# Prepare and drain steps of the second batch's attention heads, in an attention and mixture-of-experts kernel

## The chip, the core and the metric

The kernel runs on one core of a Trainium2 chip. The time is device microseconds (us) of one execution. Before the change the median of three executions is 731.03 us (730.82 to 731.37). The engines are named as in the profile: PE (matrix multiply) and PEld (its weight loads), DVE (vector), ACT (scalar), POOL (GpSimd), and SP, which issues nearly all transfers from one queue, in program order.

## What is computed

The reference runs two layers one after the other, on 2 batches of 8 heads with 768 positions of 64 columns:

```python
q_bits = (np.einsum('bhsd,dk->bhsk', q, proj) > 0)
k_bits = (np.einsum('bhsd,dk->bhsk', k, proj) > 0)
mask = q_bucket[:, :, :, None] == k_bucket[:, :, None, :]
scores = np.where(mask, scale * np.matmul(q, k.transpose(0, 1, 3, 2)), -1e9)
x = softmax(scores) @ v            # heads side by side: (1536, 512)
for e in range(4):
    out += p[:, e:e + 1] * (np.maximum(x @ w1[e], 0.0) @ w2[e])
```

The bucket of a position is a 6-bit hash of its row (the signs of its products with `proj`).

## The kernel before

**Heads and steps.** The 16 heads, counted 0 to 15 over both batches (8 to 15 are the second batch), are worked through one after the other, each in six steps, one for each 128 query rows. Step i = 6x + t is row block t of head x. Steps 96 to 108 only drain what is left. A generator (`attention`) emits the stages of a step in the order of the letters `TXSUVMEYNRP` and hands control back after each stage that has a charge. Heads 0 to 8 turn their probabilities on PE (stage T). Heads 9 to 15, which I call light, turn them by a detour: stage X (L490) turns 32x32 blocks on DVE and writes three row blocks together to a scratch in DRAM (`scr`, L496), and stage Y (L507) reads them back with four transfers into a tile `pt`. A head has two such groups of three row blocks, g0 and g1.

**The lags.** Y for g0 of head x stands in step 0 of head x+1 and Y for g1 in step 3 of head x+1. Stage V (L525, 24 matmuls) is the product with v; it needs both `pt` tiles of its head. For a light head it stands 8 steps after the head's last row block, that is in step 1 of head x+2. Stage U copies V's PSUM bank out one step later (ACT L554 for one half, DVE L552 for the other). The pool of `pt` tiles has 3 buffers, and the block-turned tile of g1 takes one of them, so Y for g0 of head x+1 needs a buffer that V of head x gives free. V stands one step behind that Y. Tiles are handed out with semaphores, so this Y simply waits on SP until PE has run V.

**Preparing a head.** `prep_head` prepares head x+1 during the first steps of head x, one piece at stage P of each step. For a light head: step 0 makes the rounded copy `ah` (ACT L330) and three copies of it on POOL; step 1 makes the rest `al` (DVE L333), then the hash: four small matmuls into `hps` (PE L346) and two sign evaluations (ACT L356); step 2 makes the bits (POOL). Heads 2 to 8 do these pieces in steps 1, 2 and 3. Block loads of the next q and k (`tqk`, L206, four transfers) are issued at step 1 of each head.

**The experts.** Once the first batch's attention is done (step 53) the first batch's expert layers start, and the second batch's attention runs between their pieces. There are 8 units, u0 to u7. A unit has 8 first-layer blocks, F0 to F7 (12 matmuls of 384 columns each, L791 to L793; ACT L797 makes `hh`, DVE L798 makes `hl`), and 6 second-layer tiles, G0 to G5 (12 matmuls of 512 columns, L731 to L733; DVE L725). Every weight comes as a 512 KB transfer (L681, issued by `load_w`) into one of two buffers `ws`; DVE rounds it (L699), POOL makes the rest (L692). `split_w` advances by one piece after each block or tile: the w2 of a unit is rounded at F0 to F3 of that unit, and its two transfers are issued after G4 and after G5 of the unit before. The w1 of the next unit is rounded at G0 to G3, its transfers are issued at F4 and F6. All of these share four one-bank PSUM buffers (`ps1`): expert blocks, `hps` and the pv bank. DVE works in program order, so what stands behind a rounding waits with it.

**The pace.** Each expert piece has a charge (1960 for F, 2600 for G), and each attention stage has one (1363 for S, 654 for T, 978 when a head is prepared, 2500 for a drain step). Attention pieces are emitted while their sum is below the experts' sum times 112,404 / 250,240 = 0.449:

```python
for c in (moe_fast if b else moe)(b, b * NU):
    dm += c
    while da < dm * ATT_PACE * n_att / n_moe:
        x = next(att, None)
        ...
        da += x
```

`n_att` counts 1632 = 654 + 978 for each prepared head, while a head's generator hands back only 978. `mixed(b, h)` is true for heads 0 to 8 (`LIGHT_FROM` is 9, `H` is 8).

Of the kernel before, what the change touches and what calls it, by code (L numbers as in the profile page):

```python
# [8 lines left out]
F32 = mybir.dt.float32  # L9
F32R = mybir.dt.float32r  # L10
ACTF = mybir.ActivationFunctionType
ALU = mybir.AluOpType
PSUM = bass.MemoryType.PSUM

P = 128
# [3 lines left out]
SGN_SCALE = float(2**20)  # L19
ATT_PACE = 1.0  # L20
LAG_E = 1
SPLIT_AT = (1, 0)
HASH_AT = (3, 1)
LAG_N = 3
LAG_R = ((6, 4), (7, 6))
LAG_T = 3
LAG_X = 2
LAG_Y = 4
LAG_V = ((4, 6), (8,))
LAST_V = (4, 5)  # L30
LAG_U = (3, 1)
LAG_M = (10, 10)
# [19 lines left out]
def tile_lsh_attention__then__domain_moe(  # L52
# [11 lines left out]
    nc = tc.nc  # L64
    B, H, S, D = q.shape
# [12 lines left out]
    NH = S // 2  # L78
# [3 lines left out]
    MKE = MK + 2 * NB  # L82
    scale = 1.0 / float(D) ** 0.5
# [21 lines left out]
    def one(name):  # L105
        return ps1.tile([P, 512], F32, tag="one", name=name)

    ident = const.tile([P, P], F32, name="ident")
    qk_scale = const.tile([P, 1], F32, name="qk_scale")
    sgn_bias = const.tile([P, 1], F32, name="sgn_bias")  # L110
# [4 lines left out]
    pf = const.tile([P, P - D], F32, name="pf")  # L115
# [6 lines left out]
    def two(t):  # L122
        return t.rearrange("p (a n) -> p a n", a=2)
# [103 lines left out]
    def stack_tiles(b, h):  # L227
        heads[b, h] = tuple(stk.tile([P, S], F32R, tag=n, name=n) for n in ("q1", "al", "ah", "k2"))
        return heads[b, h]

    def copy_pool(dst, src):
        nc.gpsimd.tensor_scalar(out=dst, in0=src, scalar1=1.0, scalar2=1.0, op0=ALU.mult, op1=ALU.mult)
# [7 lines left out]
    def split_half(dst_hi, dst_lo, src):  # L240
        nc.scalar.activation(dst_hi, src, ACTF.Copy, scale=qk_scale)
        nc.vector.scalar_tensor_tensor(
            out=dst_lo, in0=src, scalar=qk_scale, in1=dst_hi.bitcast(F32), op0=ALU.mult, op1=ALU.subtract
        )

    halves = [slice(i * NH, (i + 1) * NH) for i in range(2)]
# [54 lines left out]
    def prep_head(b, h):  # L301
        second = (b, h) == (0, 1)
        q1, al, ah, k2 = stack_tiles(b, h)

        def copies():
            for rows in (slice(0, D), slice(D, P)):
                copy_pool(q1[rows], ah[0:D].bitcast(F32))
            copy_pool(k2[0:D], ah[D:P].bitcast(F32))

        if second:  # L310
            for ps, sl in zip(in_psum, halves):
                split_half(ah[:, sl], al[:, sl], ps[:, :NH])
            copies()
            yield 654
            yield 0
            ps = [one("hps1") for _ in range(2)]
            for j, (w, a) in enumerate(((phi, ah), (plo, ah), (phi, al))):
                for i, sl in enumerate(halves):
                    nc.tensor.matmul(ps[i][:MKE, :NH], w, a[:, sl], start=j == 0, stop=j == 2)
            copy_pool(ah[0:D], al[D:P].bitcast(F32))  # L320
            for i, sl in enumerate(halves):
                nc.scalar.activation(
                    k2[D:MKE, sl], ps[i][D:MKE, :NH], ACTF.Sign, bias=sgn_bias[D:MKE], scale=SGN_SCALE
                )
            yield 978
        else:
            xt = xts.pop((b, h))
            for _ in range(SPLIT_AT[not mixed(b, h)]):
                yield 0
            nc.scalar.activation(two(ah), two(xt), ACTF.Copy, scale=qk_scale)  # L330
            copies()
            yield 0
            nc.vector.scalar_tensor_tensor(  # L333
                out=two(al),
                in0=two(xt),
                scalar=qk_scale,
                in1=two(ah).bitcast(F32),
                op0=ALU.mult,
                op1=ALU.subtract,
            )  # L340
            copy_pool(ah[0:D], al[D:P].bitcast(F32))
            for _ in range(HASH_AT[not mixed(b, h)] - SPLIT_AT[not mixed(b, h)] - 1):
                yield 0
            hps = one("hps")
            for i, sl in enumerate(halves):
                nc.tensor.matmul(  # L346
                    hps[i * D : i * D + MKE - D, :NH],
                    pf[:, : MKE - D],
                    xt[:, sl],
                    start=True,  # L350
                    stop=True,
                    tile_position=(0, i * D),
                )
            for i, sl in enumerate(halves):
                rows = slice(i * D, i * D + MKE - D)
                nc.scalar.activation(  # L356
                    k2[D:MKE, sl], hps[rows, :NH], ACTF.Sign, bias=sgn_bias[rows], scale=SGN_SCALE
                )
            if not mixed(b, h):
                yield 978  # L360
        nc.gpsimd.tensor_scalar(
            out=al[D:MKE],
            in0=k2[D:MKE].bitcast(F32),
            scalar1=1.0,
            scalar2=bit_mul[D:MKE],
            op0=ALU.add,
            op1=ALU.mult,
        )
        copy_pool(k2[MQ:MQE], al[MK:MKE].bitcast(F32))
        yield 978 if mixed(b, h) and not second else 0  # L370

    xhi = {}
    xlo = {}
# [17 lines left out]
    def mixed(b, h):  # L391
        return b * H + h < LIGHT_FROM
# [35 lines left out]
    rows = {}  # L428
# [151 lines left out]
    def v_lags(b, h):  # L580
        return LAST_V if (b, h) == (0, H - 1) else LAG_V[not mixed(b, h)]

# [6 lines left out]
    def attention():  # L589
# [3 lines left out]
        def do(op, i):  # L593
# [24 lines left out]
            elif op == "S":  # L618
                if i < n:
                    b, h, t = seq[i]  # L620
                    if t == 0:
                        x = hseq.index((b, h))
                        prep[0] = prep_head(*hseq[x + 1]) if x + 1 < len(hseq) else iter(())
                    stage_s(b, h, t)
                    return 652 + 4270 // NT
# [383 lines left out]
    with tc.manual_schedule():  # L1009
# [6 lines left out]
        i = 0  # L1016
# [57 lines left out]
```

## Time and profile before

| | us |
|---|---|
| median of 3 executions | 731.03 (730.82 to 731.37) |
| the profiled execution, its own time | 729.12 |
| its span, first to last instruction | 727.4 |
| PE busy in that span | 711.5 |
| mean granted clock of PE | 0.997 |

Up to about 130 us the first batch's attention runs, up to about 460 us the first batch's experts with the second batch's attention between them, and then the second batch's experts alone. A row with "[4.67 <-DVE hl L798]" says that the engine stood idle for 4.67 us before this instruction and what released it. "SPq" is SP's queue. [...]

### The profile page before, as it was taken

To read this page: it belongs to the slowest core of one execution; us is meant where nothing else is said; L and a number is where in the kernel's file an instruction comes from. 1 tells how busy PE (TensorE), PEld (TensorE's weight loads), DVE (VectorE), ACT (ScalarE), POOL (GpSimd) and SP (SyncE) were. 2 spreads that over 40 slices of the span, in tenths; PEclk is the share of its full clock that TensorE was granted. 3 is DMA by queue.
4 is the path that set the end of the run, shared out by engine and by line. 5 is a ranking of instruction groups with operands and counts; after the bars stand their busy time and mean duration, and the time that the engine had idled before them with its cause. 6 is when DMAs were issued, how large, how long until landed. Compare 5 with 4: busy or idle time off the path is not lost.

```text
span 727.4 us, 10195 instructions
## 1 busy us (share of the span) xinstructions
PE 711.5 (98%) x3786; PEld 602.5 (83%) x3786; DVE 483.0 (66%) x800; ACT 296.6 (41%) x588; POOL 303.0 (42%) x283
## 2 busy tenths in 40 slices
PE   8999999999999999999979999999999999999998
PEld 6766766887978878798768889898998989899896
DVE  6898898456857566668524333986768576685863
ACT  6888888432433324323111111543425334352440
POOL 6359577413354253424213243933434243342420
PEclk9999999999999999999999999999999999999999
DMA  5323253227858869786466121142113221112202
GB/s 146 66 46 88 58 117 80 39 77 187 232 138 225 234 175 236 212 267 195 134 199 163 37 71 67 59 146 87 59 59 87 58 87 58 59 59 88 87 1 87
DMA packets 88641, 83.05 MB, mean 114 GB/s; under 512 B 53008, under 2 KB 55568, under 8 KB 88592
## 3 DMA queue, kind: packets, MB, share of 16 engines
q1 hardware_dynamic: 87568, 82.08, 41.0%
q8 instruction: 30, 0.49, 0.3%
q10 hardware_dynamic: 1024, 0.33, 0.2%
q14 instruction: 19, 0.16, 0.1%
HBM read 62.68 MB, written 19.71 MB: 113 GB/s over the span
## 4 chain that ended last, share of the span: by engine, by line
PE 88%; DVE 3%; DMA 3%; ACT 2%; POOL 1%; issue 1%; SPq 1%; DVEq 0%; POOLq 0%; ACTq 0%
PE mps L731 12%; PE mps L732 12%; PE mps L733 12%; PE pv L525 8%; PE mps L791 5%; PE mps L792 5%; PE mps L793 5%; PE ptps L470 4%; PE sps L404 4%; PE sps L402 4%; DMA ws<-in_moe_w_dram 3%; PE mps L946 2%; PE mps L942 2%; PE mps L945 2%; PE pd L942 2%; PE pa L946 2%
## 5 line engine op out<-in xcount | busy, mean ns | idle before, releaser
L731 PE MATMUL mps<-w2hi,hh 128*128 128x512 f32 (+1 forms) x388 | 151.0, 389 | 0.0
L733 PE MATMUL mps<-w2hi,hl 128*128 128x512 f32 (+1 forms) x388 | 150.5, 388 | 0.0
L732 PE MATMUL mps<-w2lo,hh 128*128 128x512 f32 (+1 forms) x388 | 150.4, 388 | 0.0
L725 DVE SCALAR_TENSOR_TENSOR acc<-mps,pe,acc 128x512 f32<-128x512 f32 (+1 forms) x85 | 63.0, 741 | 70.9 <-PE mps L733 70.4
L425 ACT ACTIVATE p<-p,nb 128x768 f32<-128x768 f32 x96 | 89.5, 933 | 35.6 <-DVE p L409 35.1
L797 ACT ACTIVATE hh<-mps 128x384 fp32r<-128x384 f32 x64 | 31.4, 491 | 169.8 <-PE mps L793 169.8
L409 DVE TENSOR_SCALAR_CACHE_REDUCE p<-sps 128x768 f32<-128x768 f32 x96 | 90.3, 942 | 15.1 <-PE sps L404 13.5
L791 PE MATMUL mps<-xs,w1hi 128*128 128x384 f32 x256 | 87.6, 342 | 4.7 <-DVE hl L798 4.7
L792 PE MATMUL mps<-xs,w1hi 128*128 128x384 f32 x256 | 86.6, 338 | 0.6 <-POOL xs L570 0.6
L793 PE MATMUL mps<-xs,w1lo 128*128 128x384 f32 x256 | 86.6, 338 | 0.0
L733 PEld LDWEIGHTS mps<-w2hi,hl 128*128 128x128 f32 x388 | 72.9, 188 | 15.7
L928 POOL TENSOR_TENSOR w2lo<-ws,w2hi 128x512 fp32r<-128x512 f32 x32 | 40.6, 1289 | 108.3 <-ACT w2hi L927 108.3
L731 PEld LDWEIGHTS mps<-w2hi,hh 128*128 128x128 f32 x388 | 72.9, 188 | 15.0 <-issue 1.2
L732 PEld LDWEIGHTS mps<-w2lo,hh 128*128 128x128 f32 x388 | 72.9, 188 | 13.9
L692 POOL TENSOR_TENSOR w1lo<-ws,w1hi 128x512 fp32r<-128x512 f32 x32 | 41.2, 1290 | 84.9 <-DVE w1hi L699 76.8
L692 POOL TENSOR_TENSOR w2lo<-ws,w2hi 128x512 fp32r<-128x512 f32 x32 | 41.2, 1288 | 82.5 <-DVE w2hi L699 66.3
L798 DVE SCALAR_TENSOR_TENSOR hl<-mps,hh 128x384 fp32r<-128x384 f32 x64 | 35.4, 555 | 59.1 <-ACT hh L797 58.8
L525 PE MATMUL pv<-pt,tv 128*64 128x384 f32 x288 | 67.3, 492 | 0.0
L402 PE MATMUL sps<-ah,q 128*128 128x384 f32 x192 | 54.0, 362 | 1.8 <-DVE p L409 1.8
L791 PEld LDWEIGHTS mps<-xs,w1hi 128*128 128x128 f32 x256 | 48.6, 190 | 8.2 <-DVE hl L798 5.0
L887 POOL TENSOR_TENSOR w1lo<-ws,w1hi 128x512 fp32r<-128x512 f32 x24 | 37.1, 1547 | 36.5 <-ACT w1hi L883 22.5
L470 PEld LDWEIGHTS ptps<-ident,p 128*128 128x128 f32 x324 | 36.4, 140 | 18.3 <-ACT p L425 8.2
(137 smaller groups left out, 1392.2 us busy)
## 6 DMA issues: line engine op xcount, KB each, us to landing
ws<-in_moe_w_dram SPq DMA_DIRECT2D x64, 512.0 KB, 4.0
scr<-t SPq DMA_DIRECT2D x14, 1152.0 KB, 8.6
pt<-scr SPq DMA_DIRECT2D x56, 288.0 KB, 6.1
tv<-in_v_dram SPq DMA_DIRECT2D x16, 192.0 KB, 3.7
tqk<-in_q_dram SPq DMA_DIRECT2D x30, 96.0 KB, 3.0
out_dram<-acc SPq DMA_DIRECT2D x11, 256.0 KB, 2.0
tqk<-in_k_dram SPq DMA_DIRECT2D x28, 96.0 KB, 3.1
rdb<-row SPq DMA_DIRECT2D x14, 192.0 KB, 6.2
```

Source lines behind the costliest of these rows:

```text
L402: nc.tensor.matmul(ps[:, i, :NH], q1[:, sl], k1[:, i * NH : (i + 1) * NH], start=True, stop=False)
L409: nc.vector.tensor_scalar(out=two(pt), in0=ps[:, :, :NH], scalar1=MASKED, scalar2=MASKED, op0=ALU.min, op1=ALU.min, accum_out=nb,)
L425: nc.scalar.activation(pt, pt, ACTF.Exp, bias=nb, scale=-1.0, accum_out=dens[b, h, r][:, o : o + 1])
L470: nc.tensor.transpose(ps[:, c * P : (c + 1) * P], pt[:, (a + c) * P : (a + c + 1) * P], ident)
L525: nc.tensor.matmul(dst, vvs[b, h][:, c], pts[b, h, g][c], start=c == 0, stop=c == NT - 1, tile_position=(0, g * D),)
L692: nc.gpsimd.tensor_tensor(out=lo[:, c - 1], in0=st[c - 1], in1=hi[:, c - 1].bitcast(F32), op=ALU.subtract)
L731: nc.tensor.matmul(ps, hh[:, ts], w2hi[:, f, cs], start=n == 0, stop=False)
L732: nc.tensor.matmul(ps, hh[:, ts], w2lo[:, f, cs], start=False, stop=False)
L733: nc.tensor.matmul(ps, hl[:, ts], w2hi[:, f, cs], start=False, stop=n == FC - 1)
L791: nc.tensor.matmul(ps[:, :SB], w1hi[:, kk, fs], xhi[b, kk][:, sl], start=kk == 0, stop=False)
L792: nc.tensor.matmul(ps[:, :SB], w1hi[:, kk, fs], xlo[b, kk][:, sl], start=False, stop=False)
L793: nc.tensor.matmul(ps[:, :SB], w1lo[:, kk, fs], xhi[b, kk][:, sl], start=False, stop=kk == KD - 1)
```

## The change

Light heads get their product with v one step earlier (8 to 7 steps, so in step 0 of head x+2, where the letters put V ahead of Y), and their hash in step 0 of the preparation, between `ah` and `al`. The preparation's first piece of every head from 2 on now hands back a charge of 654 where it handed back 0. The test that chooses between the two orders of pieces is written as `b * H + h > H` where it was `not mixed(b, h)`.

```diff
-HASH_AT = (3, 1)
+HASH_AT = (3, 0)
-LAG_V = ((4, 6), (8,))
+LAG_V = ((4, 6), (7,))
...
-            for _ in range(SPLIT_AT[not mixed(b, h)]):
-                yield 0
-            nc.scalar.activation(two(ah), two(xt), ACTF.Copy, scale=qk_scale)
-            copies()
-            yield 0
-            nc.vector.scalar_tensor_tensor(
...
-            for _ in range(HASH_AT[not mixed(b, h)] - SPLIT_AT[not mixed(b, h)] - 1):
-                yield 0
-            hps = one("hps")
...
-            if not mixed(b, h):
+            late = b * H + h > H
+            steps = {}
+            steps.setdefault(SPLIT_AT[late], []).append("hi")
+            steps.setdefault(SPLIT_AT[late] + 1, []).append("lo")
+            steps.setdefault(HASH_AT[late], []).append("hash")
+            for at in range(max(steps) + 1):
+                if at:
+                    yield 654 if at == 1 else 0
+                for what in steps.get(at, ()):
+                    if what == "hi":
+                        nc.scalar.activation(two(ah), two(xt), ACTF.Copy, scale=qk_scale)
+                        copies()
+                    elif what == "lo":
...
+                    else:
+                        hps = one("hps")
...
+            if late:
                 yield 978
...
-        yield 978 if mixed(b, h) and not second else 0
+        yield 0 if second or b * H + h > H else 978
```

## Rows read from the trace of the kernel before

**Rows 1.** Page, part 1: busy time, share of the span and instructions
```profile
PE 711.5 (98%) x3786; PEld 602.5 (83%) x3786; DVE 483.0 (66%) x800; ACT 296.6 (41%) x588; POOL 303.0 (42%) x283
```

**Rows 2.** Stretches: length, busy PE, PEld, DVE, ACT, POOL, clock, DMA share, GB/s
```profile
109.00:127.00 18.00, 17.48 (x112) 11.26 (x110) 14.51 (x28) 14.91 (x32) 14.04 (x16) 1.00 0.39 82
...
273.00:291.00 18.00, 16.51 (x94) 15.90 (x93) 12.17 (x23) 7.33 (x15) 5.71 (x5) 1.00 0.95 235
...
364.00:382.00 18.00, 13.33 (x69) 12.06 (x66) 4.84 (x9) 2.34 (x5) 2.55 (x2) 0.91 0.67 201
```

**Rows 3.** Timeline of PE, 262 to 300 and 360 to 400 us: pauses, and a later matmul
```profile
285.38 0.62 PE L402 MATMUL sps<-ah,q 128*128 128x384 f32 x2 [0.29 <-DVE p L409]
289.68 0.58 PE L402 MATMUL sps<-ah,q 128*128 128x384 f32 x2 [1.21 <-DVE p L409]
...
378.56 0.66 PE L791 MATMUL mps<-xs,w1hi 128*128 128x384 f32 x1 [4.67 <-DVE hl L798]
...
382.15 0.33 PE L793 MATMUL mps<-xs,w1lo 128*128 128x384 f32 x1
```

**Rows 4.** Chain that ended last, in order of time, 361 to 378 us
```profile
361.35 4.07 PE pv L525 x24
...
368.39 9.13 DMA ws<-in_moe_w_dram
377.96 0.56 DVE hl L798
```

**Rows 5.** Timeline of all engines, 360 to 382 us
```profile
365.39 1.73 SPq L507 DMA_DIRECT2D pt<-scr  x4
...
365.93 0.33 PE L791 MATMUL mps<-xs,w1hi 128*128 128x384 f32 x1
...
368.01 0.33 PE L791 MATMUL mps<-xs,w1hi 128*128 128x384 f32 x1
...
368.39 1.60 SPq L681 DMA_DIRECT2D ws<-in_moe_w_dram  x2
...
377.62 0.43 DVE L699 CAST w2hi<-ws 128x512 fp32r<-128x512 f32 x1 [8.79 <-DMA ws<-in_moe_w_dram]
```

**Rows 6.** Waits of SP's queue: in total, times, longest, whole span
```profile
SPq L507 <- PE pv L525: 45.5, 6, 11.2
```

**Rows 7.** The stretch after the last pause, columns as in rows 2
```profile
378.50:382.00 3.50, 3.44 (x11) 3.44 (x12) 3.40 (x7) 0.00 (x0) 2.23 (x2) 0.52 0.01 2
```

**Rows 8.** Timeline of SP's queue, 250 to 283 us
```profile
250.57 2.00 SPq L507 DMA_DIRECT2D pt<-scr  x4
...
271.16 0.51 SPq L681 DMA_DIRECT2D ws<-in_moe_w_dram  x1
271.71 3.95 SPq L206 DMA_DIRECT2D tqk<-in_q_dram  x2
275.70 5.05 SPq L206 DMA_DIRECT2D tqk<-in_k_dram  x2
280.85 0.61 SPq L681 DMA_DIRECT2D ws<-in_moe_w_dram  x1
```

**Rows 9.** Chain that ended last, in order of time, 262 to 281 us
```profile
262.09 0.24 PE mps L731
...
264.85 4.07 PE pv L525 x24
...
271.16 10.02 DMA ws<-in_moe_w_dram
```

**Rows 10.** Transfers issued from 120 to 460 us: count, KB each, median us to landing
```profile
pt<-scr SPq DMA_DIRECT2D x56, 288.0 KB, 6.1
ws<-in_moe_w_dram SPq DMA_DIRECT2D x28, 512.0 KB, 6.1
```

**Rows 11.** Tile pt, its transfers from 150 to 420 us
```profile
DMA to landing us min/median/max: 3.4/6.1/8.8
```

**Rows 12.** Groups by line and form: the hash's sign evaluation, busy, mean ns, idle
```profile
L356 ACT ACTIVATE k<-hps,sgn_bias 44x384 fp32r<-44x384 f32 x28 | 16.1, 577 | 37.4 <-PE hps L346 37.2
```

More of the change, by code (lines that the diff above doesn't have):

```diff
@@ L327, in prep_head @@
             xt = xts.pop((b, h))
-            for _ in range(SPLIT_AT[not mixed(b, h)]):
-                yield 0
-            nc.scalar.activation(two(ah), two(xt), ACTF.Copy, scale=qk_scale)
-            copies()
-            yield 0
-            nc.vector.scalar_tensor_tensor(
[L334 to L340, printed above, removed]
@@ L341, in prep_head @@
-            copy_pool(ah[0:D], al[D:P].bitcast(F32))
-            for _ in range(HASH_AT[not mixed(b, h)] - SPLIT_AT[not mixed(b, h)] - 1):
-                yield 0
-            hps = one("hps")
[L345 to L358, printed above, removed]
-            if not mixed(b, h):
+            late = b * H + h > H
[3 more added lines that the diff above has]
+            steps.setdefault(HASH_AT[late], []).append("hash")
@@ new lines, in prep_head @@
+            for at in range(max(steps) + 1):
[6 more added lines that the diff above has]
+                    elif what == "lo":
+                        nc.vector.scalar_tensor_tensor(
+                            out=two(al),
+                            in0=two(xt),
+                            scalar=qk_scale,
+                            in1=two(ah).bitcast(F32),
+                            op0=ALU.mult,
+                            op1=ALU.subtract,
+                        )
+                        copy_pool(ah[0:D], al[D:P].bitcast(F32))
+                    else:
+                        hps = one("hps")
+                        for i, sl in enumerate(halves):
+                            nc.tensor.matmul(
+                                hps[i * D : i * D + MKE - D, :NH],
+                                pf[:, : MKE - D],
+                                xt[:, sl],
+                                start=True,
+                                stop=True,
+                                tile_position=(0, i * D),
+                            )
+                        for i, sl in enumerate(halves):
+                            rows = slice(i * D, i * D + MKE - D)
+                            nc.scalar.activation(
+                                k2[D:MKE, sl], hps[rows, :NH], ACTF.Sign, bias=sgn_bias[rows], scale=SGN_SCALE
+                            )
```

## The prediction

> **What bounds the kernel now.** I read the page's busy times first: PE is busy for 711.5 us, 98% of the span [rows 1]. The change takes no matmul away and adds none, so it can only win or lose in what PE does not do: its pauses, and matmuls at a low clock. Then I read a table of stretches, to see where PE pauses while the two layers run together, from 130 to 460 us. From 145 us on, two stretches are not full: 273 to 291 lacks 1.49 us, and 364 to 382 lacks 4.67 and has a mean clock of 0.91 [rows 2]. The timeline of PE shows the pauses: 0.29 and 1.21 us before a score product (S), waiting for DVE L409, and one of 4.67 us at 378.56, waiting for DVE's `hl` [rows 3].
>
> The chain of waits tells where the long one comes from. It goes from a product with v on PE (V, 361.35, 4.07 us) to a weight load issued at 368.39 that takes 9.13 us, and then DVE's `hl` and PE [rows 4]. The timeline shows the link between: SP issues Y's four reads at 365.39, just when V ends, and the two weight loads stand behind them, at 368.39. DVE had waited 8.79 us for the first of them at its rounding (377.62) [rows 5], and `hl`, which stands behind that rounding, could not give a PSUM bank free. SP stands before Y for V six times, 45.5 us in all, up to 11.2 [rows 6]. That is what the step between Y and V makes: Y for g0 of a head is in the queue one step before the V that frees its buffer, and everything behind it in SP's queue waits.
>
> **Where the change puts things.** I counted the emission by the charges. Y for g0 of head 15 is emitted once the attention's sum, 66,922, is below 0.449 of the experts' sum; that is 148,985, passed after G3 of u4 (125,120 + 15,680 + 4 x 2600 = 151,200). V of head 14 follows at 69,422, that is 154,552, after G5 (156,400). So both weight loads for u5, which are issued after G4 and G5, stand behind a Y that waits for a V behind G5. With the change heads 10 to 15 each hand back 654 more, 3,924 in all, 8,736 in the experts' charges (divided by 0.449). V and Y then stand in one step, V ahead, at 70,846, that is 157,721: after F0 of u5 (158,360). Both loads now stand ahead of this Y.
>
> The same count at the other place: Y of head 12 stands after G3 of u2 and V of head 11 after G4, so before the change the first load for u3 waits behind Y. It goes out at 271.16 and lands 10.02 us later [rows 8, 9]. The second waits further behind the q and k loads, at 271.71 and 275.70, and goes out at 280.85 [rows 8]. After it V and Y stand behind G5, so the first load is ahead of Y, and the q and k loads move from before G5 to after F2 of u3, behind the second load. For heads 9 to 13 no load stands between Y and V before the change. V itself hardly moves against the experts (two blocks or tiles later at most): the step that it gains is used up by the charge. What moves is everything else of the attention, later.
>
> **The sum, part by part.**
> - The long pause goes: -4.67 [rows 3]. The loads for u5 can go out once POOL has freed the buffers, ahead of G5 instead of at 368.39. Next in line is the rounding after F0, which would then wait at most a few us, and PE has V (4.07) [rows 4] right behind F0 to cover it. Were that cover gone, three free PSUM banks, so three F blocks of 2.08 us (12 matmuls, 365.93 to 368.01 [rows 5]), would still stand before a pause.
> - The low clock after it goes. [...] From 378.56 to 382.15 [rows 3] PE does 11 matmuls, 3.59 us; at the 2.08 us of 12 they take 1.91: -1.68.
> - The two short pauses come from a DVE that was held up by the 10.02 us load [rows 9] and had work behind it: -1.50 [rows 3]. Bounds 0 and -1.50; I take the whole, as the first load is no longer behind Y and the second no longer behind q and k.
> - The hash of light heads, earlier by a step: the same 4 matmuls and 2 evaluations of 577 ns [rows 12]. For heads 10 to 15 ACT is busy 7.33 of 18 us there [rows 2] and hides them. Head 9's stands in the first batch, at 115 to 121 us, where ACT is busy 14.91 of 18 and PE lacks 0.52 [rows 2]. The bounds are -0.52 and +1.15, both evaluations; I take 0, as the same work stays between the same neighbours. POOL's bits come later than the hash in both, and DVE's `al` has only moved behind it.
> - The remaining weight waits on DVE: 0 to one pause like the two short ones, +1.5. I take +0.5.
> - V one step nearer to the reads of its head: 0, if they land in time (second rival). U, one step behind V in both, holds the pv bank as long as before. R, N and the v loads keep their steps.
> - The attention's end: the last drain step moves by the 8,736, from G3 of u6 to F2 of u7. It is still ahead of F4 of u7, where what is left would be forced out, and the second batch's inputs are not made before F5. Cost 0; cover gone, that input work would start late on DVE.
> - The new test `b * H + h > H` picks heads 9 to 15, as `not mixed` did, so head 8's preparation keeps its pieces and steps; in the first batch nothing is paced, so its 654 does nothing.
>
> Sum: -4.67 - 1.68 - 1.50 + 0.5 = -7.35. Against the profiled execution, 729.12 us (span 727.4 and 1.72 around it), that is 721.8. This execution is 1.91 below the median of the runs, so against the median 731.03: **723.7 us**.
>
> **A rule weighed.** Two short pauses left the clock at 1.00 over the 18 us around them, the long one took it to 0.52 [rows 2, 7]; so I charge short pauses at their own length. [...]
>
> **The rivals.**
> - *The loads land late anyway.* In the new order the loads for u5 stand behind the scratch write and the reads of head 14's g1 and head 15's g0. Loads behind such traffic took 9.13 and 10.02 us [rows 4, 9] where the median is 6.1 [rows 10]. If they land as late as 377 all the same, the rounding after F0 blocks DVE, with V's bank held, and a long pause stays, whole or in part: -1.5 to -3 in all, 728 to 729.5. Against it: they are emitted after G4 and G5, which end 2.7 us before and at the start of V (361.35 [rows 4]), so 7 to 10 us ahead of 368.39. [...]
> - *V waits for its reads: slower.* The nearest case is head 11: Y for g1 is issued at 250.57 [rows 8] and V starts at 264.85 [rows 9], 14.3 us later. In the new order G3, G4, G5 and three S lie between. A G is 2.70 us (262.09 to 264.85 [rows 9] less a short gap), an S, 4 matmuls of 384 columns, a third of a block's 2.08, so 10.2 us. The four reads take 2.00 to issue [rows 8] and at worst 8.8 to land [rows 11]; from the fourth's start (1.5 in) that is 10.3. So the worst landing just about fits, the median has 2.6 to spare. It decides once reads land later than about 9 us. To end slower than before, the seven light heads would have to lose 7.35 + 1.5, about 1.3 us each (11.5 us to land): 732.5; at 2 us each with the slow clock behind three of them, 723.7 + 14 + 5 = 743. Nothing landed so late before.
> - *The change does nothing here.* If the pauses belong to the amount of traffic, and not to SP's order, they come back at other places: 730 to 731.5. Against it: the stretch with a DMA share of 0.95 lost 1.49 us, the one with 0.67 lost 4.67 [rows 2].
>
> **How the numbers follow.** My forecast, all pauses gone but for small ones (722.2 to 726): 0.75. Loads late, with part of the gain: 0.12. Nothing: 0.06. V waits, slower: 0.05. Else, 0.02. The low end is -7.85 with 0.52 and 0.5 of spread, 722.2; the high end reaches into the rival with a part of the gain, 728.2. A measurement of this kernel can tell about 0.2%, 1.5 us, from no change. Faster by more (under 729.5): 0.75 and most of 0.12, 0.87. Slower: 0.05 and a little of the rest, 0.06. The same: 0.07.
>
> **What would show it.** Right: PE lacks under 1 us in every 18 us stretch from 145 to 455; clock 1.00 there; SP's wait for V in Y has no weight load behind it that DVE then waits over 4 us for; two loads for u5 go out before V of head 14 ends. Wrong: a pause of PE over 2 us, with DVE waiting at L699 before it; V waiting for a `pt` read; PE pauses at the preparation of head 9, about 117 us.

## The result and the profile after

| | before | after |
|---|---|---|
| median of 4 executions each, us | 730.92 (730.46 to 731.37) | 722.16 (722.08 to 722.23) |
| ratio after / before | | 0.988 [0.9863, 0.9897] |
| profiled execution, its own time, us | 729.12 | 722.08 |
| its span, us | 727.4 | 720.4 |
| mean granted clock of PE | 0.997 | 1.000 |

The change makes the kernel faster by 8.76 us from median to median, and by 7.04 us from one profiled execution to the other. The forecast sum was 7.35 us. It lies between the two, and the difference between them is what much of the study is about.

In the code after the change line numbers from L346 on are up to 7 higher, so V is L532, Y is L514, weight loads are L688, and the hash is L353 (matmuls) and L363 (signs).

The first part of the page answers to [rows 1]:

```profile
PE 709.2 (98%) x3786; PEld 600.4 (83%) x3786; DVE 479.3 (67%) x800; ACT 296.6 (41%) x588; POOL 302.1 (42%) x283
```

PE has the same 3786 matmuls, busy 2.3 us less (711.5 before). The span is 7.0 us shorter, so the other 4.7 us were idle time. Next the table of stretches, with the three of [rows 2] and one more, 236 to 255 (columns as there):

```profile
109.00:127.00 18.00, 17.62 (x110) 11.01 (x108) 14.43 (x28) 14.57 (x31) 13.85 (x16) 1.00 0.37 79
236.00:255.00 19.00, 17.68 (x96) 14.32 (x93) 9.47 (x19) 7.35 (x15) 6.25 (x7) 1.00 0.73 183
273.00:291.00 18.00, 18.00 (x105) 17.98 (x104) 12.43 (x24) 7.44 (x15) 9.71 (x9) 1.00 0.91 225
364.00:382.00 18.00, 18.00 (x106) 16.11 (x103) 6.59 (x15) 3.94 (x10) 5.15 (x4) 1.00 0.69 202
```

The two stretches that were not full are full now, 18.00 of 18.00, both at clock 1.00. The new gap is in the second line: 1.32 us missing. The timeline of SP shows why the old gaps are gone (start, duration; these answer to [rows 5, 8]):

```profile
260.96 0.45 SPq L688 DMA_DIRECT2D ws<-in_moe_w_dram  x1
...
272.47 1.75 SPq L514 DMA_DIRECT2D pt<-scr  x4
274.27 0.43 SPq L688 DMA_DIRECT2D ws<-in_moe_w_dram  x1
...
353.89 3.69 SPq L688 DMA_DIRECT2D ws<-in_moe_w_dram  x2
367.02 1.75 SPq L514 DMA_DIRECT2D pt<-scr  x4
```

The two loads for u5 go out at 353.89, 13 us ahead of the Y (367.02) behind which they stood before. V of head 14 starts at 362.91, so both are out before it. For u3 the first load goes ahead of Y, the second right behind it. Two rows of the table of waits say the same (us in all, times, longest; the first answers to [rows 6]):

```profile
SPq L514 <- PE pv L532: 31.0, 6, 8.1
...
DVE w2hi L706 <- DMA ws<-in_moe_w_dram: 1.1, 1, 1.1
```

SP still waits for V six times, 31.0 us in all (45.5 before). These waits cost PE nothing: from 140 us on it waits once, 1.32 us, and that for ACT (below). What counted before was the loads that stood behind such a wait. DVE's waits for w2 loads were 20.1 us in 4 and are now 1.1 us in one.

The new gap is read from the timelines of PE and ACT at 238 to 242 us:

```profile
238.98 0.82 PE L353 MATMUL hps<-xt,pf 128*44 128x384 f32 x4
...
239.90 1.16 ACT L363 ACTIVATE k<-hps,sgn_bias 44x384 fp32r<-44x384 f32 x2 [2.51 <-PE hps L353]
...
241.11 0.44 PE L798 MATMUL mps<-xs,w1hi 128*128 128x384 f32 x1 [1.32 <-ACT k L363]
```

A first-layer block waits for the signs of a hash. ACT's L363 reads of PSUM nothing but the hash's bank, so what it releases is that bank: the block was given the bank that the hash had just used, and the hash stands right ahead of it. Clock 1.00 over 236 to 255 says that no slow stretch comes behind this pause.

The ledger from one profiled execution to the other is then -4.67 - 1.68 - 1.50 [rows 3, 7] + 1.32, and +0.18 up to 140 us (PE is idle for 6.32 us there, 6.14 before; what 109 to 127 gains, 0.14, is lost elsewhere in that part). That is -6.35 of the measured -7.04. The rest is not idle time, as from 140 us on PE has no pause but these in either kernel. Most of it is the way in which a row counts a pause. Its idle time begins at the end of the row before, which lasts 0.34 us for a first-layer matmul, while in a full stretch the next one starts 0.17 us after it. So each of the three pauses that went had cost about 0.16 us more than its row says, 0.5 in all. The last 0.2 stays open.

### The profile page after: what moved, and what is told of

It reads as the page before. It is cut to its first block, busy times and chain, and to the rows that moved or that the text cites. A ratio compares the mean times of both kernels' runs of the same rounds, so it can differ in the third digit from the quotient of the medians.

```text
span 720.4 us, 10190 instructions
## 1 busy us (share of the span) xinstructions
PE 709.2 (98%) x3786; PEld 600.4 (83%) x3786; DVE 479.3 (67%) x800; ACT 296.6 (41%) x588; POOL 302.1 (42%) x283
## 4 chain that ended last, share of the span: by engine, by line
PE 93%; ACT 2%; DVE 2%; POOL 1%; issue 1%; DMA 0%; POOLq 0%; ACTq 0%
PE mps L738 12%; PE mps L740 12%; PE mps L739 12%; PE pv L532 8%; PE mps L798 6%; PE mps L799 6%; PE mps L800 6%; PE ptps L477 4%; PE sps L411 4%; PE sps L409 4%; PE mps L953 2%; PE mps L949 2%; PE mps L952 2%; PE pd L949 2%; PE pa L953 2%; PE pa L952 2%
## 5 line engine op out<-in xcount | busy, mean ns | idle before, releaser
L532 PE MATMUL pv<-pt,tv 128*64 128x384 f32 x288 | 67.3, 492 | 0.0
```

What stands on the lines that cost most here:

```text
L532: nc.tensor.matmul(dst, vvs[b, h][:, c], pts[b, h, g][c], start=c == 0, stop=c == NT - 1, tile_position=(0, g * D),)
```

## The experiments

Theory A throughout is the prediction's: with V in the step of its Y and ahead of it, what stands behind Y in SP's queue is no longer held until a V of the next step has run, and the pauses and the low clock go. To it belongs that the 1.32 us pause is a new price, of the hash where it now stands, and that the 1.91 us between the profiled execution of before and its median were part of the same low clock. The rivals are that the charge and not V makes the gain; that the pause at 241 does not hang on the hash; and that V, once it is no longer waited for, waits itself. Each ratio is to runs of the kernel before that were made beside it; their medians are 730.09 us for the four parts, 729.99 for the next group without "both together", 730.06 for that one, and 730.27 for the last three.

### The parts of the change, one at a time

**The change with the hash one step later, as before.**

```diff
-HASH_AT = (3, 0)
+HASH_AT = (3, 1)
```

> The change with the hash put back into step 1. Theory A (the bank): the changed kernel's one new pause, 1.32 us at 241.11, comes from the hash standing right behind V of head 11's predecessor, with the next expert block given the hash's PSUM bank; with the hash back in step 1 that pause is gone and nothing else moves: 720.6 to 721.2 us. Rival (the pause belongs to this meeting of attention and experts, wherever the hash stands): 721.8 to 722.5, with a pause of over 1 us near 241. Rival 2 (the hash's earlier place is worth something): over 722.5.

Measured: 722.18 us (722.12 to 722.26), 0.9886 [0.987, 0.9903]. The pause at 241 is gone, but the time is that of the change, not the 720.6 to 721.2 expected. So the pause hangs on the hash's place, and to move the hash back gains nothing: something else takes the 1.3 us. The timeline of PE and PEld shows it. First the change, where V (24 matmuls), the hash and the next score product follow each other:

```profile
204.46 4.09 PE L532 MATMUL pv<-pt,tv 128*64 128x384 f32 x24
208.38 0.82 PE L353 MATMUL hps<-xt,pf 128*44 128x384 f32 x4
209.12 0.62 PE L409 MATMUL sps<-ah,q 128*128 128x384 f32 x2
...
209.12 0.30 PEld L409 LDWEIGHTS sps<-ah,q 128*128 128x128 f32 x2 [0.61 <-PE pv L532]
```

Then this experiment, where V stands alone and the hash alone between two second-layer tiles:

```profile
204.34 4.09 PE L532 MATMUL pv<-pt,tv 128*64 128x384 f32 x24
...
208.36 0.30 PEld L409 LDWEIGHTS sps<-ah,q 128*128 128x128 f32 x2 [0.60 <-issue]
...
211.71 0.39 PE L740 MATMUL mps<-w2hi,hl 128*128 128x512 f32 x1
212.03 0.85 PE L353 MATMUL hps<-xt,pf 128*44 128x384 f32 x4
...
212.80 0.19 PEld L738 LDWEIGHTS mps<-w2hi,hh 128*128 128x128 f32 x1 [0.62 <-issue]
212.81 0.50 PE L738 MATMUL mps<-w2hi,hh 128*128 128x512 f32 x1
213.14 0.39 PE L739 MATMUL mps<-w2lo,hh 128*128 128x512 f32 x1
213.37 0.40 PE L740 MATMUL mps<-w2hi,hl 128*128 128x512 f32 x1
```

V and the hash are 64 and 44 columns wide (128*64 and 128*44 in the rows), everything else on PE between 130 and 412 us is 128 wide (128*128 or 76*128). Behind each such narrow group here the weight loads stop for 0.60 to 0.62 us, whether it is V, the hash, or both together; it is the same behind all 11 groups of the kernel before and 10 of the 11 of the change (2.01 us at the eleventh, where the 1.32 us pause is). V and the hash together take 209.12 - 204.46 = 4.66 us. Apart they take 208.36 - 204.34 = 4.02 and, from where the next tile's matmul would have started (211.71 + the 0.23 that these are apart) to 212.81, 0.87: 4.89. The first matmul behind the hash is slow as well, 0.33 us to the next (212.81 to 213.14) where 0.23 is usual (213.14 to 213.37): 4.99. So each hash that stands beside V saves 0.33 us. In the timelines of PE between 130 and 412 us there are 11 such groups in the change, 15 in this experiment, and 11 in the kernel before, where V and hash both stood in step 1. Four more groups at 0.33 are 1.32 us, as much as the pause that went.

**V one step earlier, nothing else** (the kernel before with one number).

```diff
-LAG_V = ((4, 6), (8,))
+LAG_V = ((4, 6), (7,))
```

> The kernel before with V one step earlier and nothing else. Theory A (SP's order): V and Y stand in one step, after G3 of u4, ahead of both loads for u5, so the pause of 4.67 us and its slow clock go; the q and k loads still stand ahead of the second load for u3, so 0 to 1.5 us of short pauses stay there: 722 to 724.5 us. Rival (the charge is what removes the pause, by moving the attention): the long pause stays, 729 to 731.

Measured: 722.06 us (721.89 to 722.14), 0.9884 [0.987, 0.9899], the whole gain of the change. SP's wait for V is 30.2 us in 6, longest 6.3, and DVE's for w2 loads 7.3 us in 4, longest 3.5; no pause of PE is left at 285, 289 or 378:

```profile
273.00:291.00 18.00, 18.00 (x104) 17.96 (x103) 14.03 (x27) 6.73 (x14) 9.48 (x9) 1.00 1.02 306
364.00:382.00 18.00, 18.00 (x103) 17.76 (x102) 8.85 (x15) 3.87 (x8) 5.17 (x4) 1.00 0.76 215
```

V alone does it, and the rival that the charge does it falls. It does it in another order than the change, though: the loads for u5 still stand behind Y (359.20 and 362.20), and Y still waits for V, 6.3 us. But V now stands ahead of G4 and G5 on PE, so the loads go out 6.2 us earlier than before, DVE waits 3.5 us for the first of them where it waited 8.79, and PE does not pause. At u3 the second load still stands behind the q and k loads (268.24 and 277.58), and the short pauses are gone all the same.

**The charge alone** (the change with V and the hash at their old steps).

```diff
-HASH_AT = (3, 0)
-LAG_V = ((4, 6), (7,))
+HASH_AT = (3, 1)
+LAG_V = ((4, 6), (8,))
```

> The kernel before with the charge of 654 and nothing else, so Y waits again for a V one step behind it. By the count, Y of head 15 now stands after F0 of u5 and V of head 14 after F3, with both loads for u5 ahead: no pause there. But Y of head 12 stands after G5 of u2, ahead of the second load for u3, and V of head 11 after F2 of u3, behind the block at which DVE rounds that load. Theory A (SP's order): the pause moves to u3, about 270 to 285 us, 1 to 5 us long, with DVE waiting at the rounding over 5 us; 724 to 729 us. Rival (the pace alone does it): no pause over 1 us, 721 to 723.

Measured: 725.26 us (724.73 to 725.6), 0.9928 [0.9913, 0.9943]. With V late again, SP's queue holds a load behind Y again, at another unit. Its timelines of SP and DVE, at u3:

```profile
278.58 1.75 SPq L514 DMA_DIRECT2D pt<-scr  x4
280.37 0.43 SPq L688 DMA_DIRECT2D ws<-in_moe_w_dram  x1
...
287.33 0.43 DVE L706 CAST w2hi<-ws 128x512 fp32r<-128x512 f32 x1 [11.68 <-DMA ws<-in_moe_w_dram]
```

And what PE lost (the first row is again a block behind the signs of a hash, the other three wait for DVE):

```profile
280.52 0.44 PE L798 MATMUL mps<-xs,w1hi 128*128 128x384 f32 x1 [1.32 <-ACT k L363]
...
289.21 0.45 PE L798 MATMUL mps<-xs,w1hi 128*128 128x384 f32 x1 [0.69 <-DVE hl L805]
...
291.75 0.61 PE L409 MATMUL sps<-ah,q 128*128 128x384 f32 x2 [0.16 <-DVE p L416]
...
295.52 0.62 PE L409 MATMUL sps<-ah,q 128*128 128x384 f32 x2 [0.70 <-DVE p L416]
```

DVE waited longer here than ahead of the long pause of before (11.68 us against 8.79 [rows 5]), and PE lost far less, 0.69 + 0.16 + 0.70, at clock 1.0. The charge moves the emission to where the counting put it; it does not take the cause away. So the time of a blocked DVE is not the price. What PE has in hand meanwhile may be; these two places agree with that, but no run tests it by itself.

**The hash alone** (the change with V at 8 steps and no charge).

```diff
-LAG_V = ((4, 6), (7,))
+LAG_V = ((4, 6), (8,))
...
-                    yield 654 if at == 1 else 0
+                    yield 0
```

> The kernel before with the hash in step 0 and nothing else. Theory A: the long pause stays as it was, and the hash costs between 0 and 1.5 us or nothing: 730 to 732.5. Rival (the hash's place took part in the pause, by DVE's order): under 729.

Measured: 732.34 us (731.54 to 733.61), 1.0032 [1.0019, 1.0045], slower than before. The long pause is there, at 381.72, and the hash no longer stands beside V:

```profile
381.72 0.69 PE L798 MATMUL mps<-xs,w1hi 128*128 128x384 f32 x1 [4.63 <-DVE hl L805]
```

The hash moves to step 0 to follow V; without V's move it only adds narrow groups (15 against 11) and pauses (PE is idle for 7.3 us from 140 us on, 6.2 to 6.9 in the kernel before). The kernel before had 730.09, 728.89 to 731.63, in 9 runs beside these four.

### The new pause, and V's other side

**The hash ahead of V in the same step.** The four hash matmuls of heads 12 to 15 are emitted just before V, so that their bank is read while V runs (`hash_ps` holds what stood in the preparation).

```diff
...
                         if lag == at:
+                            x = hseq.index(bh) + 3
+                            if x > H + 3 and x < len(hseq):
+                                hash_ps(*hseq[x], xts[hseq[x]])
                             stage_v(*bh, part, len(v_lags(*bh)))
```

> The changed kernel with the four hash matmuls of heads 12 to 15 emitted just ahead of V in the same step instead of just behind it; the sign evaluations stay where they were. Theory A (the bank): V's 4 us now lie between the hash and the next expert block, so the sign evaluations are done before a block needs their bank; the 1.32 us pause at 241 goes and hash and V still stand next to each other: 720.7 to 721.2 us. Rival (the pause is not the bank's, or the time comes back elsewhere): 721.9 to 722.4.

Measured: 721.75 us (721.04 to 721.84), 0.9881 [0.9866, 0.9896]. The pause at 241 is gone; a hash now waits for DVE's `xt` instead, 0.36 us at 235.53. The time lies between what theory and rival gave. The profiled execution took 721.04, as -1.32 + 0.36 give from the change's 722.08; the other three took 0.6 to 0.8 more, which no row explains, so on the size this run decides nothing.

**The change without the charge.**

```diff
-                    yield 654 if at == 1 else 0
+                    yield 0
```

> The changed kernel with a charge of 0 in place of 654: V one step earlier and the hash beside it, with the attention paced as before. Theory A (the charge is worth nothing by itself, and a hash next to V saves 0.23 us a head, 4.02 + 0.87 apart against 4.66 together, over 4 heads): 0.9 us under the kernel with V alone, 721.0 to 721.4, unless a block meets the hash's bank again, which adds up to 1.3. Rival (the charge carries part of the gain): 723 to 726.

Measured: 720.93 us (720.64 to 721.42), 0.9872 [0.9858, 0.9887]; no pause, and faster than the change. Here both loads for u5 stand behind Y once more, as with V alone:

```profile
358.38 1.73 SPq L514 DMA_DIRECT2D pt<-scr  x4
...
361.38 1.05 SPq L688 DMA_DIRECT2D ws<-in_moe_w_dram  x2
```

It does no harm. Y waits 6.6 us for a V that ends at 358.3, and G4 and G5 keep PE busy behind it until 363.90; DVE's rounding waits 3.3 us for the load.

**Both together**, the hash ahead of V and no charge (the two diffs above).

> Both at once: the hash ahead of V and a charge of 0. With a charge of 0 no block met the hash's bank when the hash stood behind V (720.93, no pause over 0.6 us between 145 and 455). Theory A: so there is nothing left for the place ahead of V to save: 720.6 to 721.3. Rival (the sign evaluations still hold something up that no pause shows): 719.5 to 720.4.

Measured: 720.85 us (720.59 to 721.21), 0.9878 [0.986, 0.9896]. Without the charge there is nothing left for the hash's order to save.

**Y one step later instead of V one earlier** (the kernel before with one number).

```diff
-LAG_Y = 4
+LAG_Y = 5
```

> The kernel before with Y one step later (lag 5), so that it stands in V's step, and nothing else. Theory A (SP waits at Y for a later V): V keeps its step, and the long pause goes all the same, as both loads for u5 are now out in time (the first ahead of Y, the second right behind V); some 1.5 to 3 us of short pauses stay at u3, where the second load still stands behind the q and k loads: 722.5 to 725.5. Rival (V itself had to move): 729 to 731.

Measured: 727.86 us (725.64 to 731.33 in 10 runs), 0.997 [0.9955, 0.9985], slower than the 722.5 to 725.5 expected. It also brings Y and V into one step, so the long pause goes, and so do the short ones; but now the reads go out late, and V waits for them. Its timeline of PE has two such waits:

```profile
208.54 5.42 PE L525 MATMUL pv<-pt,tv 128*64 128x384 f32 x21 [2.58 <-DMA pt<-scr]
...
303.02 3.73 PE L525 MATMUL pv<-pt,tv 128*64 128x384 f32 x21 [0.77 <-DMA pt<-scr]
```

And a stretch around the first, with the granted clock 0.65 in the third column from the end:

```profile
208.00:211.00 3.00, 2.46 (x10) 1.33 (x12) 0.11 (x1) 0.00 (x0) 1.47 (x2) 0.65 1.07 250
```

This is the prediction's slower rival, made real: V 2.58 us late, and matmuls at the low clock behind it. It takes back most of what the freed queue gave.

### The 1.91 us: the kernel before, profiled again

Three more profiled executions of the unchanged kernel.

> The kernel before once more, for a second look at its long pause. Theory A (what the first profile of it had too little of is the slow clock): pause of 4.5 to 4.9 us again, but the stretch at 0.5 behind it is about twice the 3.5 us of the first profile, 6.5 to 7.5 us, and the time 730 to 731. Rival (the pause itself varies): a pause over 5.5 us and the same 3.5 us at the low clock.

> The kernel before, a third look for an execution with a mean clock of 0.995, which most of its timed runs have. Theory A (the runs differ in how long the clock stays low behind the same pause): the pause is again 4.6 to 4.8 us; a mean clock of 0.995 comes with 6 to 8 us at the low clock, one of 0.997 or 0.998 with 3 to 4.5. Rival (they differ in the length of the pause): a pause over 5.5 us where the time is over 730.

> The kernel before, a fourth look, with the same two expectations as the third: the same pause of 4.6 to 4.8 us and a low clock whose length goes with the mean clock (theory A), or a longer pause where the time is longer (rival).

Measured: 729.56, 730.50 and 729.94 us, at mean clocks 0.998, 0.995 and 0.997. The timeline of PE in the third of the four executions (that of the prediction counted first):

```profile
285.81 0.62 PE L402 MATMUL sps<-ah,q 128*128 128x384 f32 x2 [0.67 <-DVE p L409]
...
290.10 0.59 PE L402 MATMUL sps<-ah,q 128*128 128x384 f32 x2 [1.21 <-DVE p L409]
...
379.35 0.69 PE L791 MATMUL mps<-xs,w1hi 128*128 128x384 f32 x1 [5.00 <-DVE hl L798]
...
384.52 0.34 PE L792 MATMUL mps<-xs,w1hi 128*128 128x384 f32 x1
```

The row of its stretch 378 to 384 has clock 0.50 throughout:

```profile
378.00:384.00 6.00, 4.66 (x15) 4.66 (x16) 5.51 (x10) 0.35 (x1) 3.42 (x3) 0.50 0.13 36
```

From 379.35 to 384.52 PE does 16 matmuls in 5.17 us; at the 2.08 us of 12 they take 2.77, a loss of 2.40. In the first execution the loss was 1.68 [rows 3]. The long pause of the second and of the fourth:

```profile
379.14 0.45 PE L791 MATMUL mps<-xs,w1hi 128*128 128x384 f32 x1 [4.66 <-DVE hl L798]
...
379.45 0.69 PE L791 MATMUL mps<-xs,w1hi 128*128 128x384 f32 x1 [4.65 <-DVE hl L798]
```

All four, every number read or worked out in this way:

| execution | own time | long pause | slow matmuls | short pauses | sum of the three | time less the sum |
|---|---|---|---|---|---|---|
| first | 729.12 | 4.67 | 1.68 | 1.50 | 7.85 | 721.27 |
| second | 729.56 | 4.66 | 1.68 | 1.87 | 8.21 | 721.35 |
| fourth | 729.94 | 4.65 | 1.50 | 1.86 | 8.01 | 721.93 |
| third | 730.50 | 5.00 | 2.40 | 1.88 | 9.28 | 721.22 |

Between the first and the third the time differs by 1.38 us, and the three terms by 1.43. In three of the four what is left agrees within 0.13 us; the fourth has 0.6 us that these terms do not hold. So what varies between these two is in the terms that the change removes, half of it in the slow matmuls and half in the pauses. Neither expectation came out as it was put: no stretch at the low clock was as long as 6 us (5.0 us in the third), and no pause was over 5.5. The timed runs agree: of the 35 runs of before beside the experiments, 25 have a mean clock of 0.995 and a mean time of 730.40 us, 10 have 0.997 and 729.60. Kernels without the long pause (the change, V alone, no charge) have 0.999 or 1.000, and the runs of each lie within 0.8 us of each other.

### Three versions on one chip

The change, the change without the charge, and V alone, each as above, with 7 shared runs of the kernel before (730.27, 729.43 to 731.12).

> The changed kernel again, on one chip with the next two. By the sums so far (a pause of 1.32 us where a block meets the hash's bank, less 0.23 us for each of four hashes next to V): 0.2 to 0.5 us above the kernel with V alone, and 1.0 to 1.4 above the one with a charge of 0. Rival (the pause at 241 costs nothing in the end, and the runs of different jobs differed by their chips): within 0.3 us of the one with a charge of 0.

> V one step earlier, the hash beside it, a charge of 0, on one chip with the changed kernel and with V alone. By the sums so far: 0.7 to 1.1 us under V alone (0.23 us for each of four hashes next to V), 1.0 to 1.4 under the changed kernel. Rival (chips differ, the hash's place is worth nothing): within 0.3 us of V alone.

> V one step earlier and nothing else, on one chip with the two others. By the sums so far between them: 0.2 to 0.5 us under the changed kernel and 0.7 to 1.1 above the one with a charge of 0. Rival: all three within 0.3 us of each other.

| | median, us | range | ratio | hash beside V | pause behind the hash |
|---|---|---|---|---|---|
| the change | 722.14 | 722.12 to 722.42 | 0.9889 [0.9874, 0.9903] | yes | 1.32 us |
| without the charge | 720.71 | 720.64 to 720.77 | 0.9868 [0.9853, 0.9883] | yes | none |
| V alone | 722.18 | 721.89 to 722.54 | 0.9888 [0.9871, 0.9904] | no | none |

The change has its pause again, at 241.41:

```profile
241.41 0.44 PE L798 MATMUL mps<-xs,w1hi 128*128 128x384 f32 x1 [1.32 <-ACT k L363]
```

The version without the charge has none. Two of its stretches, to be held against those of the change:

```profile
236.00:255.00 19.00, 19.00 (x103) 17.99 (x102) 12.61 (x24) 8.35 (x18) 6.50 (x7) 1.00 1.02 254
...
364.00:382.00 18.00, 18.00 (x103) 17.70 (x102) 9.17 (x16) 3.94 (x8) 5.17 (x4) 1.00 0.78 220
```

So the charge costs 1.43 us, of which the pause is 1.32. The hash beside V is worth 1.47 us, of which four groups less are 1.32. In the change the two cancel, which is why it measures the same as V alone. The expectations had wanted 0.2 to 0.5 us between those two, as they counted a group at 0.23, without the slow matmul behind it. V one step earlier, the hash beside it and no charge is the best version here, ahead of both kernels.

## Why the prediction was right, and where it was wrong

**The mechanism was right.** Nothing late stands behind Y, the long pause and the low clock behind it are gone, and so are the two short pauses. V alone brings the whole gain of the change, and Y one step later takes the long pause away as well, from the other side. The counting of what is emitted where came out for both units, and for the charge alone it named the unit to which the wait moved. But more was put into the order than it needs: without the charge the loads stand behind Y, and at u3 the second behind q and k, and no pause comes of it. That V runs earlier than G4 and G5, and with it Y, was enough. (The sentence that for heads 9 to 13 no load stands between Y and V leaves out head 11, for which the prediction itself counts one.)

**The step that failed is the last of the sum**: "This execution is 1.91 below the median of the runs, so against the median 731.03: 723.7 us." It treats the 1.91 us as something that both kernels have. The change's profiled execution lies 0.08 us from its median, so the offset is not common. Most of it belongs to the terms that the change removes. The long pause, the matmuls behind it and the short pauses are 7.85 us in the execution that I costed and 9.28 in another of the same kernel, 1.43 us more. With the larger values the sum is -5.00 - 2.40 - 1.88 + 0.5 = -8.78, and 730.92 - 8.78 = 722.14, against 722.16 measured. That it comes so close is luck: from that execution's own 730.50 the same sum gives 721.7, and the 0.42 between it and the median is not explained; the kernel before had medians of 729.99 to 730.27 beside the experiments, and the change gained 8.13 us there. Against the profiled execution, my 721.8 stood 0.3 from the 722.08 found. The trace had a hint: a mean clock below 1 in a single execution, and a time under the shortest of the runs shown. I had one price for a term that varies, and none of the spread at the low end was for it: the measured 722.16 lies just under that end, 722.2 (722.16 before rounding).

**The hash at 0: right in its sum, wrong in its parts.** I bounded it by two sign evaluations where ACT is full, in the first batch, and said that ACT hides those of heads 10 to 15. The first batch gained 0.14 at 109 to 127, the stretch that I bounded, and nothing over its whole length. The cost came where I had put none: the signs of one hash hold a PSUM bank that PE wants next, 1.32 us, though ACT is busy for only 7.35 of 19 us there. That is over the 1 us that I allowed in any stretch. ACT's busy share was the wrong row to ask; who gets the bank next was the question. Against it stands a gain that I did not see, as I did not ask what a hash costs PE when it stands alone. Before, V and the hash stood in the same step; V's move alone parts them, and the hash's move brings them together again. Behind V, the hash, or both the weight loads stop for 0.60 to 0.62 us, and a hash that stands by itself costs PE 0.33 us more than one beside V (4.99 us for the two against 4.66). Why they stop was not shown.

**The charge** I costed at 0, by the attention's end. It shifts where a hash meets a block, and that costs 1.43 us. It was not needed: without it the loads stand behind Y, and reach DVE in time all the same.

**+0.5 for DVE's remaining waits**: 1.1 us of waiting, and no pause of PE that it ends. By name this term was too large by 0.5; in size it stood in for part of the 1.32.

**The weighed rule.** I charged short pauses at their own length. The pauses that are left, 1.32 us in the change and the four shown of the run with the charge alone, left the clock at 1.00 (over 236 to 255 us in the one, as the mean of the run in the other). So none of them brought a slow stretch like the 1.68 us behind the long pause of before.

**The rivals.** The loads land in time (DVE waits 1.1 us). "V waits for its reads" does not decide in the change, but it is real: Y one step later shows it, 2.58 us with the clock at 0.65 behind. (The 11.5 us to land that I named for it counts from the first read's issue; from the fourth's, as in the line before, it is 10.) "The change does nothing here" falls with V alone.

## What to carry to other kernels

In a queue that is worked through in order, look for the instruction that waits on a semaphore and price what stands behind it, not the wait; then bring what it waits for ahead of it, and forward on the engine that makes it. Before a sum is set against a median, compare the mean clock and the time of the profiled execution with those of the other runs: what differs may be the very term that the change removes. When work for one bank moves, ask which instruction gets that bank next, and when matmuls of another width move, whether they still stand together.

## What the runs showed of the hardware

- Behind the same pause (4.65 to 5.00 us) the matmuls at the low clock (0.52 over 378.50 to 382 us in the first execution [rows 7], 0.50 over 378 to 384 in the third) cost 1.50, 1.68, 1.68 and 2.40 us in four executions of one kernel. What makes this vary was not shown.
- Behind pauses up to 1.32 us the clock stayed at 1.00, in the change (236 to 255 us) and with the charge alone (mean of the run). One of 2.58 us, before V, was followed by 0.65 over 208 to 211 us.
- Between a group of matmuls 64 or 44 columns wide and the next weight load of 128 columns lay 0.60 to 0.62 us (21 of the 22 groups of the kernel before and the change), and a hash that stood by itself cost PE 0.33 us more than one beside V.
- DVE blocked for 11.68 us cost PE 1.55 us in pauses at one place; blocked for 8.79 us it cost 4.67 and a slow stretch at another.

Left open: the 0.2 us of the ledger that no row holds, the 0.6 us of the fourth execution, the 0.15 us between the hash's count and its measure, the 0.42 us between the third execution and the median, and the size at which the hash ahead of V came out. That PE's bank at 241 was the hash's is read from the releaser alone; the banks themselves are not in the trace.
